# The front's work in another order: q copied three steps ahead, k'v one step sooner, gating begun once its tiles are done

## The chip, the cores and the metric

The kernel runs on one core of a Trainium2 chip. The core has a matrix engine (TensorE, PE in the rows; PEld is its load of weights), VectorE (DVE), ScalarE (ACT), GpSimd (POOL) and SyncE (SP), which only issues DMAs here. Each engine works off its own queue strictly in order and waits for the others through semaphores. The metric is the device time of one execution in microseconds, lower is better.

## The reference

```python
# attention: 4 batches, 8 heads, 576 rows, head dimension 64, float32
kv  = einsum('bhsd,bhse->bhde', k, v)
out = einsum('bhsd,bhde->bhse', q, kv)
out = out / sqrt(mean(out*out, -1) + 1e-6) * g_norm
x   = out.transpose(0, 2, 1, 3).reshape(2304, 512)
# mixture of experts: 8 experts, width 1024, the best two of each row
noisy = x @ w_gate + log1p(exp(x @ w_noise)) * noise
x = sum over the two best e of  weight_e * (relu(x @ w1[e]) @ w2[e])
# MLP of width 2048
h = maximum(x @ w_in, 0)
out = (s * h*h + b) @ w_out
```

## The kernel before

The 2304 rows are 18 tiles of 128. The program has two parts. The **front** does the attention, the norm and the gating and writes normalised rows to a table xs in HBM. The **main part** gathers the rows of each expert from xs, multiplies, and ends with the MLP. Every product of the main part is made of three fp32r matmuls (L815 to L817 and L839 to L841), with each operand split into a high and a low part (xh and xl, w1h and w1l, w2h and w2l, hh and hl).

The order of work is written out by hand: each engine's queue holds its instructions in the order in which the code emits them, and SyncE's DMAs go out in that order too. The change is all in the front, which runs over ten chunks, or **steps**, c = 0 to 9. A step has two tiles, or one (steps 4 and 9, which hold the last 64 rows of two batches each). Steps 0 and 1 are batch 0, 2 and 3 batch 1, 5 and 6 batch 2, 7 and 8 batch 3; step 4 needs batches 0 and 1, step 9 batches 2 and 3. What is emitted for a chunk:

- **repack(c)** copies q of chunk c into qc, heads in the order of the transposes: on ScalarE for odd c, on VectorE for even c (L398, L400). **q_tr(c)** transposes qc on TensorE (L410, into qtp), and ScalarE evicts to qT (L412).
- **kv(b)** multiplies k' by v of batch b (L334) and ScalarE evicts to kvc (L339). **kv_put(b)** copies kvc into the block-diagonal kvbd on VectorE (L345). **mfold_a(b)** transposes kvc (L352, evicted to kvT, L354); **mfold_b(b)** multiplies it by the gate's weights (L361) and ScalarE puts the result beside kv in kvbd (L364). att of a batch needs both.
- **att(c, u)** multiplies qT by kvbd for tile u (L423), and **evict(c, u)** takes it to x on ScalarE (L432). **squares(c)** (sq, ScalarE, L438), **sums(c)** (ss, VectorE, L445; iw, GpSimd, L447), **inv_rms(c)** (iv, two ScalarE instructions, L457 and L458) and **norm(c)** (six VectorE instructions, L469 to L479: iu twice, iv, x's gate columns, the logits lg, the normalised xn) make the norm. **put_rows** writes xn to xs with a DMA on SyncE (L487).
- **advance(n)**, from step 6 on, loads expert weights on SyncE and splits n units: w1h and w2h on ScalarE, w1l on VectorE, w2l on GpSimd (L154).

**Gating** of the first nine tiles is a generator that tick() moves on. Each tick either runs its next piece or counts down the number that the last piece yielded; norm has five ticks, one behind each of its last five instructions (iu is two), sums has one. Its pieces: gate_noise (two ScalarE, two GpSimd instructions, from lg; yields 2), gate_choice twice (six VectorE instructions each, beginning with m_all, L518; 1 each), a pause of 6, gate_rank (matmuls; 1), the one-hots (nine VectorE instructions, L540; 6), the matmuls of the list of rows (L546; 1), the list idx_e (VectorE, L550) and two gathers from xs on GpSimd (L187; 11), and put_x for the two blocks gathered: four transposes (L371), xh on ScalarE (L374), xl on VectorE (L375). What is left at the end of the front is run at once by finish_chain. Then the first expert's matmuls start (L815 to L817).

Tiles rotate through buffers: x has two (a chunk's evict waits for norm of the chunk two before it), xn three (norm waits for the DMA of the chunk three before), q, k and v two batches each (a load waits for the last reader), qc and qT two, qtp one.

Of the kernel before, what the change touches and what calls it, by code (L numbers as in the profile page):

```python
# [8 lines left out]
F32 = mybir.dt.float32  # L9
# [12 lines left out]
def kernel(  # L22
# [18 lines left out]
    P = 128  # L41
    B, H, S, D = q.shape
# [23 lines left out]
    HW_ = D + W2C  # L66
# [146 lines left out]
    pool = front.__enter__()  # L213
# [4 lines left out]
    def small_ps(shape):  # L218
        p_, tag, bufs = small[0]
        return p_.tile(shape, F32, name="sps", tag=tag, bufs=bufs)  # L220
# [4 lines left out]
    def load_kv(b, m0=0, m1=NM):  # L225
        for nm, src in (("k", k), ("v", v)):
            sv = src[b].rearrange("h s d -> (h s d)").rearrange("(m r x) -> r m x", r=P, x=KJ * D)
            if m0 == 0:
                KQV[b, nm] = pool.tile([P, NM, KJ, D], F32, name=nm, bufs=2)
            nc.sync.dma_start(KQV[b, nm].rearrange("p m j d -> p m (j d)")[:, m0:m1], sv[:, m0:m1])  # L230


    def load_q(b):
        KQV[b, "q"] = pool.tile([P, H, NJ, D], F32, name="q", bufs=2)
        nc.sync.dma_start(KQV[b, "q"].rearrange("p h j d -> p h (j d)"),
                          q[b, :, :SM].rearrange("h (p j) d -> p h (j d)", j=NJ))
        if b % 2 == 0:
            KQV[b // 2, "qr"] = pool.tile([P, H, D], F32, name="qr", bufs=2)
        o = SR * (b % 2)
        nc.sync.dma_start(KQV[b // 2, "qr"][o:o + SR], q[b, :, SM:].rearrange("h p d -> p h d"))  # L240
# [101 lines left out]
    def kv_put(b):  # L342
        for m in range(2):
            r = slice(m * D, (m + 1) * D)
            nc.vector.tensor_copy(kvbd[b][r, :, :, m, :D], KVP[b][1][r])  # L345


    def mfold_a(b):
        kvc = KVP[b][1]
        pt = small_ps([P, 2, P])  # L350
        for a in range(2):
            nc.tensor.transpose(pt[:, a, :], kvc[:, a].rearrange("p i d -> p (i d)"), ident)  # L352
        kvT = pool.tile([P, 2, P], F32, name="kvT", bufs=1)
        nc.scalar.activation(kvT, pt, AF.Copy)  # L354
        KVP[b] = kvT

    def mfold_b(b):
        kvT = KVP[b]
        pm = small_ps([P, 2, 2, 2, W2C])
        for a in range(2):  # L360
            nc.tensor.matmul(pm[:, a], lhsT=kvT[:, a, :], rhs=gw[:, a], start=True, stop=True)  # L361
        for m in range(2):
            r = slice(m * D, (m + 1) * D)
            nc.scalar.activation(kvbd[b][r, :, :, m, D:], pm[r, :, m], AF.Copy)  # L364
# [12 lines left out]
    QC, QT, AT, XC, XO = {}, {}, {}, {}, []  # L377
# [8 lines left out]
    def repack(c):  # L386
        if c >= NCH:
            return
        t0, n = CHUNKS[c]
        qc = QC[c] = pool.tile([P, 2, 2, 2, 2, D], F32, name="qc", bufs=2)  # L390
        for u in range(n):
            tl = TILES[t0 + u]
            src = KQV[tl[0], "q"][:, :, tl[1], :] if n == 2 else KQV[tl[0] // 2, "qr"]
            src = src.rearrange("p (a m i) d -> p i a m d", a=2, m=2)
            for i in range(2):
                dst = qc[:, u, :, i]
                if c % 2:
                    nc.scalar.activation(dst, src[:, i], AF.Copy)  # L398
                else:
                    nc.vector.tensor_copy(dst, src[:, i])  # L400

    def q_tr(c):
        if c >= NCH:
            return
        t0, n = CHUNKS[c]
        qc = QC.pop(c).rearrange("p u a i m d -> p u (a i) (m d)")
        pt = fps.tile([P, 2, 4, P], F32, name="qtp", bufs=1)
        for u in range(n):
            for g in range(4):
                nc.tensor.transpose(pt[:, u, g, :], qc[:, u, g, :], ident)  # L410
        qT = pool.tile([P, 2, 4, P], F32, name="qT", bufs=2)
        nc.scalar.activation(qT[:, :n], pt[:, :n], AF.Copy)  # L412
        QT[c] = qT
# [14 lines left out]
    def evict(c, u):  # L428
        t0, n = CHUNKS[c]
        if u == 0:  # L430
            XC[c] = (pool.tile([P, 2, H, HW_], F32, name="x", bufs=2),)
        nc.scalar.activation(XC[c][0][:, u].rearrange("p (a h) c -> p a h c", a=2), AT.pop(t0 + u), AF.Copy)  # L432

    def squares(c):
        x, = XC[c]
        n = CHUNKS[c][1]
        sq = pool.tile([P, 2, H, D], F32, name="sq", bufs=1)
        nc.scalar.activation(sq[:, :n], x[:, :n, :, :D], AF.Square)  # L438
        XC[c] = (x, sq)

    def sums(c):
        x, sq = XC[c]
        n = CHUNKS[c][1]
        ss = pool.tile([P, 2, H], F32, name="ss", bufs=2)
        nc.vector.tensor_reduce(ss[:, :n], sq[:, :n], axis=AX, op=OP.add)  # L445
        w = pool.tile([P, 2, H], F32, name="iw", bufs=2)
        nc.gpsimd.tensor_scalar(w[:, :n], ss[:, :n], -0.5 / D, -0.5e-6, op0=OP.mult, op1=OP.add)  # L447
        tick()
        XC[c] = (x, ss, w)

    def inv_rms(c):
        if c < 0:
            return
        x, ss, w = XC[c]
        n = CHUNKS[c][1]
        y = pool.tile([P, 2, H], F32, name="iv", bufs=2)
        nc.scalar.activation(y[:, :n], ss[:, :n], AF.Ln, scale=1.0 / D, bias=eps)  # L457
        nc.scalar.activation(y[:, :n], y[:, :n], AF.Exp, scale=-0.5)  # L458
        XC[c] = (x, w, y)

    def norm(c):
        if c < 0:
            return
        x, w, y = XC.pop(c)
        t0, n = CHUNKS[c]
        x, w, y = x[:, :n], w[:, :n], y[:, :n]

        u = pool.tile([P, 2, H], F32, name="iu", bufs=2)[:, :n]
        nc.vector.tensor_mul(u, y, y)  # L469
        nc.vector.tensor_mul(u, u, w)  # L470
        tick()
        nc.vector.scalar_tensor_tensor(y, u, 1.5, y, op0=OP.add, op1=OP.mult)
        tick()
        nc.vector.tensor_mul(x[:, :, :, D:], x[:, :, :, D:], y[:, :, :, None].to_broadcast([P, n, H, W2C]))
        tick()
        nc.vector.tensor_reduce(lg[:, t0:t0 + n, :], x[:, :, :, D:].rearrange("p n h c -> p n c h"), axis=AX, op=OP.add)
        tick()
        xn = pool.tile([P, 2, H, D], F32, name="xn", bufs=3)[:, :n]
        nc.vector.tensor_mul(xn, x[:, :, :, :D], y[:, :, :, None].to_broadcast([P, n, H, D]))  # L479
        tick()  # L480
        XO.append((t0, n, xn))

    def put_rows():
        if not XO:
            return
        t, n, x = XO.pop(0)
        nc.sync.dma_start(xs[t * P:(t + n) * P, :].rearrange("(n p) d -> p n d", n=n), x.rearrange("p n h d -> p n (h d)"))  # L487
# [9 lines left out]
    def gate_noise(g):  # L497
        t0, t1 = GROUPS[g]
        T = t1 - t0
        ex = gate_tmp(g, [P, T, E])  # L500
        nc.scalar.activation(ex, lg[:, t0:t1, E:], AF.Exp)
        nc.scalar.activation(ex, ex, AF.Ln, bias=ones1)
        nl = gate_tmp(g, [P, T, E])
        nc.gpsimd.tensor_mul(nl, ex, nz[:, t0:t1, :])
        nc.gpsimd.tensor_add(nl, nl, lg[:, t0:t1, :E])
        GT[g] = (nl, gate_tmp(g, [P, T, E]), gate_tmp(g, [P, T, E], BF16))
        yield 2
# [92 lines left out]
    def gating(g):  # L600
        yield from gate_noise(g)
        yield from gate_choice(g, 0)
        yield from gate_choice(g, 1)
        yield 6
        yield from gate_rank(g)
        yield from gate_slots(g)
# [4 lines left out]
    def tick():  # L611
        if chain[0] is None:
            return
        if chain[1] > 1:
            chain[1] -= 1
            return
        chain[1] = next(chain[0], None)
        if chain[1] is None:
            chain[0] = None
# [115 lines left out]
    repack(1)  # L735
    q_tr(1)
    load_q(2)

    KV_AT = {1: 1, 3: 2, 6: 3}

    for c, (t0, n) in enumerate(CHUNKS):
        new = KV_AT.get(c)
        for u in range(n):
            att(c, u)
            evict(c, u)
            if u == 0:
                inv_rms(c - 1)
        if new:
            kv(new)
        squares(c)  # L750
        repack(c + 2)
        q_tr(c + 2)
        if new:
            kv_put(new)
            mfold_a(new)
        norm(c - 1)
        put_rows()
        sums(c)
        if new:
            mfold_b(new)  # L760
        if c == 1:
            load_kv(3)
            load_q(3)
        if c and sum(CHUNKS[c - 1]) == NT0:
            chain[:] = [gating(0), 0]
        if c >= 6:
            advance(c - 6)
    inv_rms(NCH - 1)
# [345 lines left out]
```

## Time and profile before

| | |
|---|---|
| time of three runs | 1008.91 us median (1008.45 to 1009.35) |
| the profiled execution | 1007.86 us, span of its trace 1006.1 us |
| PE matmul busy | 948.1 us, 94% of the span |
| DVE, ACT, POOL busy | 530.0, 397.3 and 109.8 us |
| DMA | 129.03 MB, mean 128 GB/s |

The span runs from the first to the last instruction. Busy time is the time in which an engine had an instruction in work; a matmul's end is modelled. In a row of a timeline, "x4" says that several like instructions are merged, and the bracket at the end gives how long the engine stood idle before it and what released it.

### The profile page before, as it was taken

To read this page: it belongs to the slowest core of one execution; us is meant where nothing else is said; L and a number is where in the kernel's file an instruction comes from. 1 tells how busy PE (TensorE), PEld (TensorE's weight loads), DVE (VectorE), ACT (ScalarE), POOL (GpSimd) and SP (SyncE) were. 2 spreads that over 40 slices of the span, in tenths; PEclk is the share of its full clock that TensorE was granted. 3 is DMA by queue.
4 is the path that set the end of the run, shared out by engine and by line. 5 is a ranking of instruction groups with operands and counts; after the bars stand their busy time and mean duration, and the time that the engine had idled before them with its cause. 6 is when DMAs were issued, how large, how long until landed. Compare 5 with 4: busy or idle time off the path is not lost.

```text
span 1006.1 us, 14220 instructions
## 1 busy us (share of the span) xinstructions
PE 948.1 (94%) x5530; PEld 821.8 (82%) x5531; DVE 530.0 (53%) x976; ACT 397.3 (39%) x708; POOL 109.8 (11%) x128
## 2 busy tenths in 40 slices
PE   6763799999999999999999999999999999999997
PEld 4753688888999999999998998888878878887886
DVE  1458667554576776776745565434434443443333
ACT  2565243433464565555534443322223232222222
POOL 2002134300010010000000112100110011000000
PEclk8787699999999999999999999999999999999999
DMA  9824386825478466675635532200120012001001
GB/s 287 288 90 157 107 261 198 274 72 182 136 231 280 148 219 211 215 260 170 224 116 189 177 128 82 74 11 1 36 91 1 22 47 58 1 1 42 1 1 42
DMA packets 103354, 129.03 MB, mean 128 GB/s; under 512 B 9808, under 2 KB 68176, under 8 KB 103280
## 3 DMA queue, kind: packets, MB, share of 16 engines
q1 hardware_dynamic: 95856, 108.02, 32.6%
q0 software_dynamic: 6208, 20.00, 6.9%
q8 instruction: 44, 0.72, 0.3%
q14 instruction: 30, 0.25, 0.1%
q10 hardware_dynamic: 1216, 0.03, 0.1%
HBM read 92.91 MB, written 35.13 MB: 127 GB/s over the span
## 4 chain that ended last, share of the span: by engine, by line
PE 75%; DVE 1%; ACT 1%; issue 0%; ACTq 0%
PE ph L816 12%; PE ph L817 12%; PE ph L815 12%; PE y L839 12%; PE y L840 12%; PE y L841 12%; PE sps L371 2%; DVE r L825 0%; ACT hh L827 0%; ACT r L824 0%; DVE r L826 0%; DVE xl L375 0%; DVE hl L828 0%; DVE rows L848 0%; ACT xh L374 0%
## 5 line engine op out<-in xcount | busy, mean ns | idle before, releaser
L816 PE MATMUL ph<-xl,w1h 128*128 128x320 f32 (+3 forms) x832 | 278.2, 334 | 2.8 <-DVE xl L375 2.7
L817 PE MATMUL ph<-xh,w1l 128*128 128x320 f32 (+3 forms) x832 | 277.9, 334 | 2.9 <-DVE w1l L148 2.9
L815 PE MATMUL ph<-xh,w1h 128*128 128x320 f32 (+3 forms) x832 | 278.0, 334 | 2.1 <-ACT xh L374 1.2
L839 PE MATMUL y<-w2h,hh 128*128 128x512 f32 x608 | 243.4, 400 | 2.9 <-ACT hh L827 2.1
L840 PE MATMUL y<-w2l,hh 128*128 128x512 f32 x608 | 238.4, 392 | 0.0
L841 PE MATMUL y<-w2h,hl 128*128 128x512 f32 x608 | 238.2, 392 | 0.0
L816 PEld LDWEIGHTS ph<-xl,w1h 128*128 128x128 f32 x832 | 158.2, 190 | 18.5 <-DVE xl L375 5.1
L815 PEld LDWEIGHTS ph<-xh,w1h 128*128 128x128 f32 x832 | 158.2, 190 | 18.3 <-ACT xh L374 3.4
L817 PEld LDWEIGHTS ph<-xh,w1l 128*128 128x128 f32 x832 | 158.2, 190 | 12.9 <-DVE w1l L148 3.1
L819 ACT ACTIVATE hh<-ph 128x320 fp32r<-128x320 f32 (+2 forms) x128 | 55.9, 437 | 232.2 <-PE ph L817 219.9
L825 DVE SCALAR_TENSOR_TENSOR r<-ph,r 128x512 f32<-128x512 f32 (+1 forms) x80 | 51.1, 638 | 178.1 <-ACT r L824 174.0
L820 DVE SCALAR_TENSOR_TENSOR hl<-ph,hh 128x320 fp32r<-128x320 f32 (+2 forms) x128 | 62.4, 489 | 148.4 <-ACT hh L819 141.9
L841 PEld LDWEIGHTS y<-w2h,hl 128*128 128x128 f32 x608 | 114.6, 188 | 25.4 <-DVE hl L828 0.6
L839 PEld LDWEIGHTS y<-w2h,hh 128*128 128x128 f32 x608 | 114.9, 189 | 24.3 <-ACT hh L827 2.7
L840 PEld LDWEIGHTS y<-w2l,hh 128*128 128x128 f32 x608 | 115.0, 189 | 20.4
L824 ACT ACTIVATE r<-ph 128x512 f32<-128x512 f32 (+1 forms) x80 | 44.4, 556 | 190.0 <-PE ph L817 183.5
L827 ACT ACTIVATE hh<-r 128x512 fp32r<-128x512 f32 (+1 forms) x80 | 47.1, 589 | 101.6 <-DVE r L826 99.3
L828 DVE TENSOR_TENSOR hl<-r,hh 128x512 fp32r<-128x512 f32 (+1 forms) x80 | 51.1, 639 | 52.5 <-ACT hh L827 49.7
L187 POOL DMA_INDIRECT rows<-xs,idx x35 | 34.4, 982 | 314.5 <-PE sps L371 191.9
L187 POOL DMA_INDIRECT rows<-ys,slot_i x36 | 35.0, 971 | 272.5 <-DVE rows L797 136.3
L148 DVE SCALAR_TENSOR_TENSOR w1l<-raw,gcol,w1h 128x512 fp32r<-128x512 f32 x64 | 47.7, 747 | 22.1 <-ACT w1h L146 17.6
L153 ACT ACTIVATE w2h<-raw 128x512 fp32r<-128x512 f32 x80 | 49.7, 621 | 5.5 <-DMA raw<-in_moe_w_dram 5.4
(165 smaller groups left out, 807.3 us busy)
## 6 DMA issues: line engine op xcount, KB each, us to landing
raw<-in_moe_w_dram SPq DMA_DIRECT2D x128, 256.0 KB
ys<-rows SPq DMA_DIRECT2D x40, 256.0 KB
c_raw<-in_moe_w_in_dram SPq DMA_DIRECT2D x16, 512.0 KB
c_raw<-in_moe_w_out_dram SPq DMA_DIRECT2D x16, 512.0 KB
wd<-c_fl SPq DMA_DIRECT2D x16, 512.0 KB
raw<-wd SPq DMA_DIRECT2D x32, 256.0 KB
ys<-zero SPq DMA_DIRECT2D x13, 512.0 KB
q<-in_q_dram SPq DMA_DIRECT2D x4, 1024.0 KB
```

The source lines that it names most:

```text
L153: nc.scalar.activation(h2, r2, AF.Copy)
L187: nc.gpsimd.indirect_dma_start(out=dst, out_offset=None, in_=src, in_offset=bass.IndirectOffsetOnAxis(ap=icol, axis=0))
L815: nc.tensor.matmul(ps[:, :wd], lhsT=w1h[:, c, :], rhs=xh[:, c, cs], start=c == 0, stop=False)
L816: nc.tensor.matmul(ps[:, :wd], lhsT=w1h[:, c, :], rhs=xl[:, c, cs], start=False, stop=False)
L817: nc.tensor.matmul(ps[:, :wd], lhsT=w1l[:, c, :], rhs=xh[:, c, cs], start=False, stop=c == KC - 1)
L819: nc.scalar.activation(hh[:, cs], ps[:, :wd], AF.Relu)
L820: nc.vector.scalar_tensor_tensor(hl[:, cs], ps[:, :wd], 0.0, hh[:, cs].bitcast(F32), op0=OP.max, op1=OP.subtract)
L825: nc.vector.scalar_tensor_tensor(r[:, :wd], ps[:, :wd], 0.0, r[:, :wd], op0=OP.max, op1=OP.mult)
L828: nc.vector.tensor_sub(hl[:, cs], r[:, :wd], hh[:, cs].bitcast(F32))
L839: nc.tensor.matmul(y, lhsT=hh[:, cs], rhs=w2h, start=f == 0, stop=False)
L840: nc.tensor.matmul(y, lhsT=hh[:, cs], rhs=w2l, start=False, stop=False)
L841: nc.tensor.matmul(y, lhsT=hl[:, cs], rhs=w2h, start=False, stop=f == nf - 1)
```

## The change

x gets a third buffer. repack(2) is emitted ahead of the loop, and step c copies chunk c+3 behind its q_tr(c+2), where it copied chunk c+2 ahead of it. kv(b) is emitted in steps 0, 3 and 5 (before: 1, 3 and 6), behind squares in place of ahead of it, and mfold_b(b) one step after kv(b), behind that step's att. The loads of batch 3 are issued in step 0 ahead of put_rows, where they were at the end of step 1. Gating is started in step 5 ahead of sums, with one tick of its own, where it was started behind sums.

```diff
     def evict(c, u):
         t0, n = CHUNKS[c]
         if u == 0:
-            XC[c] = (pool.tile([P, 2, H, HW_], F32, name="x", bufs=2),)
+            XC[c] = (pool.tile([P, 2, H, HW_], F32, name="x", bufs=3),)
...
     load_q(2)
-
-    KV_AT = {1: 1, 3: 2, 6: 3}
+    repack(2)
+
+    KV_AT = {0: 1, 3: 2, 5: 3}
 
     for c, (t0, n) in enumerate(CHUNKS):
-        new = KV_AT.get(c)
+        new, last = KV_AT.get(c), KV_AT.get(c - 1)
         for u in range(n):
             att(c, u)
             evict(c, u)
             if u == 0:
                 inv_rms(c - 1)
+        if last:
+            mfold_b(last)
+        squares(c)
         if new:
             kv(new)
-        squares(c)
-        repack(c + 2)
         q_tr(c + 2)
+        repack(c + 3)
         if new:
             kv_put(new)
             mfold_a(new)
+        if c == 0:
+            load_kv(3)
+            load_q(3)
         norm(c - 1)
         put_rows()
-        sums(c)
-        if new:
-            mfold_b(new)
-        if c == 1:
-            load_kv(3)
-            load_q(3)
         if c and sum(CHUNKS[c - 1]) == NT0:
             chain[:] = [gating(0), 0]
+            tick()
+        sums(c)
         if c >= 6:
             advance(c - 6)
```

## Rows read from the trace of the kernel before

**Rows 1.** Busy us by stretch: total, PE, PEld, DVE, ACT, POOL, clock, DMA, GB/s

```profile
27.20:107.00 79.80, 48.58 (x687) 42.92 (x687) 50.78 (x121) 43.60 (x93) 10.14 (x17) 0.78 0.55 181
...
107.00:1006.10 899.10, 881.92 (x4643) 767.17 (x4643) 475.62 (x836) 345.71 (x600) 92.12 (x90) 0.99 0.37 119
```

**Rows 2.** Waits of VectorE, 27 to 107 us: total, times, longest

```profile
DVE kvbd L345 <- ACT kvc L339: 13.5, 3, 6.2
...
DVE iu L469 <- ACT iv L458: 9.3, 4, 4.7
DVE xl L375 <- ACT xh L374: 1.9, 1, 1.9
DVE m_all L518 <- POOL g L505: 1.8, 1, 1.8
```

**Rows 3.** Waits of TensorE for copied q, same stretch and columns

```profile
PE qtp L410 <- ACT qc L398: 13.8, 4, 6.1
```

**Rows 4.** Timeline, steps 0 to 5: start, duration, instruction, idle before

```profile
25.71 0.70 ACT L432 ACTIVATE x<-att 128x640 f32<-128x640 f32 x1 [0.38 <-PE att L423]
...
27.22 0.90 DVE L400 COPY qc<-q 128x256 f32<-128x256 f32 x4 [9.72 <-DMA q<-in_q_dram]
...
32.49 2.44 PE L334 MATMUL sps<-v,k 64*64 64x64 f32 x144
...
35.44 0.59 DVE L345 COPY kvbd<-kvc 64x256 f32<-64x256 f32 x2 [6.19 <-ACT kvc L339]
...
41.44 4.03 PE L423 MATMUL att<-kvbd,qT 128*128 128x160 f32 x16 [0.64 <-issue]
...
45.13 0.17 DVE L469 TENSOR_TENSOR iu<-iv 128x16 f32<-128x16 f32 x1 [4.67 <-ACT iv L458]
...
50.87 0.59 DVE L345 COPY kvbd<-kvc 64x256 f32<-64x256 f32 x2 [1.72 <-ACT kvc L339]
```

**Rows 5.** Timeline, steps 6 and 7

```profile
73.27 0.59 DVE L345 COPY kvbd<-kvc 64x256 f32<-64x256 f32 x2 [5.56 <-ACT kvc L339]
...
76.78 0.23 DVE L518 TENSOR_REDUCE m_all<-g 128x9 f32<-128x72 f32 x1 [1.76 <-POOL g L505]
...
81.36 1.21 DVE L445 TENSOR_REDUCE ss<-sq 128x16 f32<-128x1024 f32 x1
...
83.19 0.17 DVE L469 TENSOR_TENSOR iu<-iv 128x16 f32<-128x16 f32 x1 [0.62 <-ACT iv L458]
...
85.99 1.21 DVE L445 TENSOR_REDUCE ss<-sq 128x16 f32<-128x1024 f32 x1
...
87.59 2.87 DVE L540 TENSOR_SCALAR ohe<-io,early 128x256 f16<-128x256 f16 x9
```

**Rows 6.** Timeline, end of the front, start of the first expert

```profile
95.84 1.27 POOL L154 TENSOR_TENSOR w2l<-raw,w2h 128x512 fp32r<-128x512 f32 x1
...
95.94 1.21 DVE L470 TENSOR_TENSOR iu<-iu,iw 128x16 f32<-128x16 f32 x1
...
97.07 0.15 DVE L550 TENSOR_SCALAR idx_e<-sps 128x2 int32<-128x2 f32 x1
...
97.50 1.27 POOL L187 DMA_INDIRECT rows<-xs,idx_e  x1 [0.38 <-DVE iv L472]
...
99.07 1.34 POOL L187 DMA_INDIRECT rows<-xs,idx_e  x1 [0.30 <-issue]
...
101.04 1.21 DVE L470 TENSOR_TENSOR iu<-iu,iw 128x8 f32<-128x8 f32 x1
...
104.52 1.09 PE L371 MATMUL sps<-ident,rows 128*128 128x128 f32 x4 [2.10 <-DMA rows<-xs,idx_e]
...
107.02 0.58 PE L816 MATMUL ph<-xl,w1h 128*128 128x256 f32 x1
```

**Rows 7.** SyncE's queue of DMA issues

```profile
38.96 0.37 SPq L487 DMA_DIRECT2D xs<-xn  x1
...
41.60 4.03 SPq L240 DMA_DIRECT2D qr<-in_q_dram  x1
```

## Prediction

> **What bounds the kernel now.** I read the busy times by stretch first. After 107 us TensorE is busy 881.9 of 899.1 us at a granted clock of 0.99 [rows 1]: the experts and the MLP are bound by their matmuls, and no instruction in them changes. They start when the first gathered rows have been turned into xh and xl; the first matmul that reads xl (L816) begins at 107.02 [rows 6]. So the question is only when that moment comes. Before it, from 27.2 to 107, no engine is full: TensorE 48.6, VectorE 50.8, ScalarE 43.6 of 79.8 us [rows 1]. The time goes into handing over.
>
> VectorE has the most work there and ends last, so I keep its account: its waits in that stretch add up to 13.5 (kvbd, for kvc) + 9.3 (iu, for iv) + 1.9 (xl) + 1.8 (m_all) = 26.5 us; the 9.72 for q ended at 27.22 [rows 2, 4]. Busy 50.8 + waits 26.5 = 77.3; the other 2.5 us are short gaps between its 121 instructions, which I keep. What the change can give is in those 26.5 us.
>
> Where they come from: step 1 lasts from 29.4 to att(2) at 41.44 [rows 4]. TensorE does att(1), then k'v of batch 1 at 32.49; q_tr(3) waits for a copy of q that ScalarE makes only after kvc and squares; then come mfold_a and mfold_b, and only then att(2). TensorE waited 13.8 us in four such places for copied q [rows 3]. VectorE meanwhile stood 6.19 us before kvbd and 4.67 before iu [rows 4]; step 6 repeats it (5.56) [rows 5]. After 76.8 its waits are short (0.62 before iu at 83.19, 1.9 before xl [rows 2, 5]): there the others wait for it.
>
> **The change part by part.** No instruction and no transfer is added or removed but for a third x buffer. Every term is a wait that goes, stays or comes. I laid each engine's queue out in the new order, an instruction starting when its engine is free and its inputs are there, with the durations of the trace (TensorE's between its two clocks: 1.1 times the fast ones). The old order laid out so has att(2) at 41.2 and L816 at 106.5, where the trace has 41.44 and 107.02 [rows 4, 6]; I trust it to about 1 us.
>
> *q copied three steps ahead.* repack(2) still waits for q to land at 27.2. From repack(3) on, the copy is made a step before its transposes, in time that ScalarE has free (43.6 of 79.8 us busy); TensorE's 13.8 us go. Without that cover each copy would cost its 0.9 to 1.3 us again.
>
> *k'v one step sooner.* kv(1) runs on TensorE after att(0), whose second evict starts at 25.71, while q is still under way: 25.7 to 28.2 (2.44 us by its row). kvc is there when VectorE leaves repack(2) at 28.1, and the wait of 6.19 goes. As ss(0) ends at 30.0 and iv comes after the next evict, which stands behind qT(2) and repack(3) on ScalarE, norm(0) starts at 33.1: a new wait of 2.7. mfold_b now follows the next step's att and no longer waits for kvT ahead of it. att(2) moves from 41.4 to 34.1.
>
> In the steps that follow, VectorE runs norm (2.8 us, from 83.19 to 85.99) and ss (1.2), and then waits for one round trip: ss ends at 82.57, the next norm starts at 83.19, 0.62 us [rows 5]. I count 0.7 in front of norm(1), (3), (5) and (6): 2.8, where the row of iu had 9.3.
>
> kv_put still stands ahead of norm on VectorE, so norm and ss wait behind it, and x's buffer with them. In step 3 kvc(2) comes after sq(3), at 44.6, and VectorE is free at 42.7: 1.9 (before 1.72 [rows 4]). In step 5 att(5) starts at 50.2, kvc(3) is there at 56.1, VectorE free at 54.1: 2.0 (before 5.56).
>
> *x in three buffers.* ScalarE waited in places for xn to free x. In the new layout this is worth nothing: the same step's inv_rms waits for a later VectorE instruction anyway. Without it the layout ends at the same time; the bound is one evict, 0.7 us.
>
> *Gating begun sooner.* gate_noise now runs at the end of step 5; ScalarE waits there for lg(4), to 58.3, with evict(6) behind it: 0.5 us, off VectorE's path. Its results are on hand at 59.8, VectorE comes to the choice at 61.0, and the 1.76 before m_all [rows 5] go. The one-hots (2.87 [rows 5]) move ahead of xn(6): same work, earlier, and x waits for them. The list of rows is ready at 80.0 in place of 97.07, and the gathers go out at 80.2 and 81.5. The second one's rows reached TensorE 5.45 us after its issue (99.07 to 104.52 [rows 6]), so by 87.0; VectorE reaches put_x after lg(9), at 91.0. The gather is hidden with 4 us to spare, the 1.9 before xl goes, and xl stands ahead of xn(9). The price: iw(8) is now queued behind both gathers (1.27 + 1.34 us [rows 6]) on GpSimd, and norm(8) waits for it: 1.4.
>
> *VectorE and GpSimd.* The two-input L470 took 1.21 us at 95.94 and ended as w2l did (95.84 + 1.27); its like took 0.17, and L470 at 101.04 again 1.21 [rows 5, 6]. So two were held. Now all three splits in the front fall on a norm, since the one-hots no longer cover the first: a third hold, 1.0 to 1.1; bounds 0 and 1.27.
>
> The Trainium skill, "SBUF — State Buffer", section "Who interferes with whom", says that a VectorE instruction with two SBUF inputs and a GpSimd instruction that reads SBUF share a read port, and that the later one is blocked until the first ends. The trace agrees: 1.21 against 0.17 us. By it the third hold costs 1.1; if the splits missed the norms, as one did before, the sum would be 1.1 us better.
>
> *SyncE.* The loads of k, v, q of batch 3 now go out ahead of the first xs write, which before was issued at 38.96, right ahead of them; the last of them took 4.03 us to issue at 41.60 [rows 7]. They start at about 30, when kv(1) and repack(3) have freed the buffers, land by about 48, and nothing needs them before 51. xs(0) goes out behind them at about 41 and should have landed near 50; norm(3) needs its xn buffer at about 51.5. Bounds: nothing, or 4.5 us if it lands as late as 56. I take nothing.
>
> **Sum.** Waits 26.5 before; after, 2.7 + 2.8 + 1.9 + 2.0 + 1.4 = 10.8, and 1.1 more for holds. Gain 26.5 - 10.8 - 1.1 = 14.6 us: L816 at 92.4. From there the experts are shifted as they are: their loads are issued relative to their own steps, and three weight units are split beforehand as now. Span 1006.1 - 14.6 = 991.5; the profiled run 1007.86 - 14.6 = 993.3; the median of the runs shown is 1.05 above that run, so **994.3**.
>
> **The rivals.**
> *Half of it* (0.18). The waits for kvc, behind which all of norm stands, stay as they were: 13.5 in place of 3.9, gain 5.0, 1003.9; the late xs(0) alone would give 998.8. For it: kv_put has not moved on VectorE, and step 3 keeps its wait by my own account. Against it: TensorE no longer waits for q ahead of kv.
> *More* (0.10). The splits miss the norms and iw(8) is not late: another 2 to 3 us, about 991; with the 2.7 of norm(0) gone too, 989. For it: before, one split in three missed. No more than 26.5 us can go at all.
> *It does not do what it says* (0.05). The waits come back elsewhere on VectorE, which has 50.8 + 2.5 us of work at the least, or the experts wait for weights what the front has saved: 1008 to 1010. For it: SyncE's weight loads in the front wait for VectorE's norm. Against it: those move along with it.
> *Slower* (0.05). The experts start after a longer stretch in which TensorE is idle, and run at the lower clock for longer. The front has a mean granted clock of 0.78, the rest 0.99 [rows 1]. A stretch of t us at half the clock costs t/2, so it eats the gain when the lower level lasts 29 us longer than now; 35 us give 1012. Against it: the matmuls that follow are dense as before.
>
> **Numbers.** The forecast holds 0.62. Under 0.2% (2 us) a measurement of this kernel can't be told from no change. Faster: 0.62 + 0.18 + 0.10 = 0.90; same 0.05; slower 0.05. The forecast's own range is 991 to 998 (1 us for the layout, 0 to 4.5 for xs(0), about 2.5 the other way). With "more" down to 989 and most of "half of it" up to 1003, the range is 989 to 1003.
>
> **What would show it.** att(2) at about 34 in place of 41.4, att(7) at 61 to 62; no wait over 1 us for copied q after step 1; kvbd's waits near 0, 2 and 2; the gathers issued about 80, with put_x not waiting for a DMA; L816 near 92. If xn waits for a DMA in step 4, the order on SyncE did it; if kvbd's waits stay over 5, the first rival; if L816 comes early and the end does not follow, the third.

## The result, and the profile after

The changed kernel took 993.87 us (median of four runs, 991.76 to 996.30), the kernel before 1008.68 beside it: a ratio of 0.9855 [0.9831, 0.988], so about 14.6 us faster (14.8 by the medians). The forecast was 994.3. The profiled execution took 993.72 us with a span of 991.9; the prediction had 991.5 for the span. Line numbers up to the loop are as before; behind it they are 2 higher, so the matmul that reads xl is L818 where it was L816.

The windows of the changed kernel come first, cut at the moments that answer to [rows 1] (the start of repack(2), the first matmul that reads xl, the end); the columns are as there.

```profile
26.68:93.46 66.78, 42.47 (x612) 36.63 (x603) 50.21 (x120) 43.13 (x93) 9.93 (x17) 0.82 0.67 214
93.46:991.90 898.44, 881.58 (x4643) 766.93 (x4643) 476.20 (x837) 346.49 (x600) 92.02 (x90) 0.99 0.37 119
```

The main part takes what it took: 898.4 us after 899.1, at the same clock. The front is 13.0 us shorter (66.8 after 79.8), and VectorE's work in it is nearly the same (50.2 after 50.8). So the time came out of waits, as told, and nothing of it was given back by the experts. Of the 14.2 us between the two spans, 1.2 lie outside the front: repack(2) starts 0.5 us sooner, and the main part is 0.7 shorter.

VectorE's waits in that stretch (total, times, longest), to set against [rows 2]:

```profile
DVE iu L469 <- ACT iv L458: 5.6, 5, 3.1
DVE kvbd L345 <- ACT kvc L339: 4.5, 3, 2.0
DVE qc L400 <- PE qtp L410: 2.8, 1, 2.8
DVE iu L470 <- issue: 1.0, 1, 1.0
DVE iv L472 <- DVE iu L470: 0.3, 1, 0.3
```

They add up to 14.2 us (the wait for q ahead of 26.68 is left out as before), where they were 26.5. The 1.0 that the view calls "issue" ends when GpSimd's iw(8) does, at 85.0; in other runs of this order the view names it (L447). The waits for m_all and for xl are gone. One line is new, and the prediction has nothing like it: VectorE waits 2.8 us to copy q, for TensorE's transposes. The timeline of steps 0 to 2 shows where (start, duration, instruction, idle before and releaser, as in [rows 4]):

```profile
25.35 2.33 PE L334 MATMUL sps<-v,k 64*64 64x64 f32 x144
...
27.61 0.66 PE L410 MATMUL qtp<-ident,qc 128*128 128x128 f32 x4
...
28.21 0.59 DVE L345 COPY kvbd<-kvc 64x256 f32<-64x256 f32 x2 [0.63 <-ACT kvc L339]
...
31.68 1.11 PE L410 MATMUL qtp<-ident,qc 128*128 128x128 f32 x4 [3.42 <-issue]
...
32.84 0.49 DVE L400 COPY qc<-qr 128x256 f32<-128x256 f32 x2 [2.79 <-PE qtp L410]
...
36.42 0.17 DVE L469 TENSOR_TENSOR iu<-iv 128x16 f32<-128x16 f32 x1 [3.09 <-ACT iv L458]
...
37.42 2.41 PE L423 MATMUL att<-kvbd,qT 128*128 128x160 f32 x16
```

kv(1) runs in step 0 and its kvbd waits 0.63 us, where that wait was 6.19. q_tr(2) then stops in its middle: four of its eight transposes run, TensorE does nothing for 3.42 us, and the profile finds no instruction that it waited for ("issue"). All eight read what VectorE had copied by 27.6. q_tr(2) ends 3.4 us later for it, VectorE's copy of the last 64 rows of batches 0 and 1 (into the buffer that q_tr(2) frees) waits 2.79 us, and att(2) comes at 37.42 where the prediction had 34.1.

The rest of the front, from the start of gating to the first expert:

```profile
61.54 0.26 ACT L501 ACTIVATE g<-lg 128x72 f32<-128x72 f32 x1 [0.64 <-DVE lg L476]
...
64.23 0.22 DVE L518 TENSOR_REDUCE m_all<-g 128x9 f32<-128x72 f32 x1
...
73.38 1.85 DVE L540 TENSOR_SCALAR ohe<-io,early 128x256 f16<-128x256 f16 x9
...
81.94 0.15 DVE L550 TENSOR_SCALAR idx_e<-sps 128x2 int32<-128x2 f32 x1
...
83.76 0.98 POOL L187 DMA_INDIRECT rows<-xs,idx_e  x1 [0.30 <-issue]
...
85.10 1.26 POOL L154 TENSOR_TENSOR w2l<-raw,w2h 128x512 fp32r<-128x512 f32 x1
...
85.26 1.13 DVE L472 SCALAR_TENSOR_TENSOR iv<-iu,iv 128x16 f32<-128x16 f32 x1
...
89.05 1.09 PE L371 MATMUL sps<-ident,rows 128*128 128x128 f32 x4 [0.47 <-DMA rows<-xs,idx_e]
...
92.13 1.28 DVE L375 TENSOR_TENSOR xl<-sps,xh 128x512 fp32r<-128x512 f32 x2
...
93.46 0.58 PE L818 MATMUL ph<-xl,w1h 128*128 128x256 f32 x1 [2.06 <-DVE xl L375]
```

m_all has its input when VectorE comes to it. The nine one-hots take 1.85 us in place of 2.87 [rows 5]. The second block's rows reach TensorE 5.3 us after the gather was issued, and VectorE takes both xl without a wait.

### The profile page after: what moved, and what is told of

It reads as the page before. It is cut to its first block, busy times and chain, and to the rows that moved or that the text cites. A ratio compares the mean times of both kernels' runs of the same rounds, so it can differ in the third digit from the quotient of the medians.

```text
span 991.9 us, 14216 instructions
## 1 busy us (share of the span) xinstructions
PE 943.4 (95%) x5530; PEld 818.1 (82%) x5531; DVE 530.1 (53%) x976; ACT 397.3 (40%) x708; POOL 109.5 (11%) x128
## 4 chain that ended last, share of the span: by engine, by line
PE 76%; DVE 1%; ACT 1%; issue 0%; ACTq 0%
PE ph L818 13%; PE ph L819 13%; PE ph L817 12%; PE y L841 12%; PE y L843 12%; PE y L842 12%; PE sps L371 2%; DVE r L827 0%; ACT hh L829 0%; ACT r L826 0%; DVE r L828 0%; DVE xl L375 0%; DVE hl L830 0%; DVE rows L850 0%; ACT xh L374 0%
## 5 line engine op out<-in xcount | busy, mean ns | idle before, releaser
L818 PE MATMUL ph<-xl,w1h 128*128 128x320 f32 (+3 forms) x832 | 278.2, 334 | 4.7 <-DVE xl L375 4.7
L818 PEld LDWEIGHTS ph<-xl,w1h 128*128 128x128 f32 x832 | 158.0, 190 | 20.5 <-DVE xl L375 6.9
```

Of the source, the lines that this page charges most:

```text
L818: nc.tensor.matmul(ps[:, :wd], lhsT=w1h[:, c, :], rhs=xl[:, c, cs], start=False, stop=False)
```

## The experiments

All ratios are to the kernel before on the same chip, with 95% intervals. Executions start their loads a little earlier or later, so the profiled runs are compared by the stretch from repack(2) on VectorE to the first matmul that reads xl ("front" below). That is one execution of each kernel; the two of the changed kernel differ by 1.3 us:

| kernel | repack(2) | first xl matmul | front, us | ratio |
|---|---|---|---|---|
| before | 27.22 | 107.02 | 79.8 | 1 |
| changed | 26.68 | 93.46 | 66.8 | 0.9855 [0.9831, 0.988] |
| changed, again | 25.13 | 90.66 | 65.5 | 0.9859 [0.984, 0.9878] |
| copy_only | 26.29 | 96.51 | 70.2 | 0.9897 [0.9879, 0.9915] |
| kv_only | 25.58 | 98.97 | 73.4 | 0.9919 [0.9904, 0.9934] |
| gate_only | 27.16 | 108.01 | 80.9 | 0.9997 [0.9986, 1.0009] |
| gate_late | 26.78 | 100.95 | 74.2 | 0.9931 [0.9915, 0.9946] |
| x_two | 26.06 | 94.01 | 68.0 | 0.9876 [0.9855, 0.9898] |
| load2_late | 26.50 | 95.53 | 69.0 | 0.9871 [0.9847, 0.9895] |
| load2_wait | 25.82 | 93.74 | 67.9 | 0.9869 [0.9852, 0.9886] |
| load2_pool | 26.82 | 95.30 | 68.5 | 0.9872 [0.9851, 0.9893] |
| low_dve | 27.66 | 93.30 | 65.6 | 0.9867 [0.9846, 0.9889] |
| put_late | 27.04 | 90.19 | 63.2 | 0.9832 [0.981, 0.9855] |
| put_late_load2 | 25.93 | 88.76 | 62.8 | 0.9813 [0.9791, 0.9835] |

### One part alone

**The copies alone, three steps ahead, in the kernel before.**

```diff
     load_q(2)
+    repack(2)
...
-        repack(c + 2)
         q_tr(c + 2)
+        repack(c + 3)
```

> The kernel before with q alone copied three steps ahead. My theory (VectorE's waits for what TensorE and ScalarE hand over are what goes, and the parts share them): TensorE no longer waits for copied q ahead of its transposes, so most of the way to the whole gain: 8 to 10 us of the 14.6, some 1000 us, kvbd's wait of 5 to 6 us shrinks as steps get shorter, the gather is still waited for. Rival (each part has its own waits, and they add up): a third or less, 1004 us.

It gave 994.43 us, 0.9897: 10.5 us, just above the 8 to 10 expected. VectorE's waits in its front, to set against [rows 2]:

```profile
DVE kvbd L345 <- ACT kvc L339: 9.3, 3, 6.0
DVE iu L469 <- ACT iv L458: 3.1, 3, 1.8
DVE m_all L518 <- POOL g L505: 2.4, 1, 2.4
DVE xl L375 <- ACT xh L374: 2.0, 1, 2.0
```

TensorE's waits for copied q are gone, and with them most of VectorE's waits for iv (3.1 after 9.3). The wait for kvc in step 1 stays at 6.0: the copies do not free it. Some of that 6.0 is a stop of TensorE of 1.6 us inside kv(1), which a later section takes up.

**k'v alone, one step sooner, its folds spread.**

```diff
-    KV_AT = {1: 1, 3: 2, 6: 3}
+    KV_AT = {0: 1, 3: 2, 5: 3}
...
-        new = KV_AT.get(c)
+        new, last = KV_AT.get(c), KV_AT.get(c - 1)
...
+        if last:
+            mfold_b(last)
+        squares(c)
         if new:
             kv(new)
-        squares(c)
...
-        if new:
-            mfold_b(new)
```

> The kernel before with k'v one step sooner and mfold_b behind the next step's att, alone. My theory: also 6 to 9 us by itself, 1000 to 1003 us, so that the two parts done singly give more together than the whole change, because both shorten the same steps. Rival: 4 us or less, as the copy of q still holds TensorE.

It gave 996.58 us, 0.9919: 8.4 us. Here it is the other way round: kvbd waits 5.7 us in all and 2.7 at most, iu 9.0 in all and 4.5 at most, and TensorE's waits for copied q are back at 14.7. The two parts take different waits, each mainly what the prediction gave it: the copies those for iv, k'v those for kvc.

**Gating alone, begun sooner, in the kernel before.**

```diff
+        if c and sum(CHUNKS[c - 1]) == NT0:
+            chain[:] = [gating(0), 0]
+            tick()
         sums(c)
...
-        if c and sum(CHUNKS[c - 1]) == NT0:
-            chain[:] = [gating(0), 0]
```

> The kernel before with gating begun sooner, alone. Taken out of the changed kernel, it cost some 7 us. Theory (its worth there is that copies of q and k'v, moved sooner on ScalarE, stood ahead of gate_noise and kept VectorE waiting; without them there is little to win): within 2 us of the kernel before, on either side. Rival (the parts add up, and gating sooner hides the gather by itself): 5 to 7 us faster than the kernel before.

It gave 1005.16 us beside 1005.76: 0.9997 [0.9986, 1.0009], no change. The waits before m_all and xl do go (1.8 and 1.9 us, [rows 2]), but VectorE now waits 1.9 for the matmuls that rank the tiles (L565) and 1.0 for iw(8) behind the gathers. It comes to m_all at 76.79, as before (76.78), though it no longer waits there: kvbd's waits are 2.0 longer, 1.3 of it in step 3, ahead of any gating, in a stretch in which this execution had the lower clock for longer (0.73 from 40 to 55 us, where the kernel before had 0.84). TensorE stops in it as well, for 1.71 us inside kv(1), though the order up to there is that of the kernel before, whose trace has no such stop:

```profile
34.59 0.56 PE L334 MATMUL sps<-v,k 64*64 64x64 f32 x20 [1.71 <-issue]
```

**The changed kernel with gating begun as before.**

```diff
-        if c and sum(CHUNKS[c - 1]) == NT0:
-            chain[:] = [gating(0), 0]
-            tick()
         sums(c)
+        if c and sum(CHUNKS[c - 1]) == NT0:
+            chain[:] = [gating(0), 0]
```

> The changed kernel with gating begun where the kernel before begins it. My theory: VectorE's list of rows and the gathers come a step later and the gather's way (5 us) stands again ahead of xl: 2 to 3 us slower than the changed kernel, 996 to 997 us. Rival (gating is hidden in any case, the gain is all in the steps): no difference.

It gave 998.16 us, 0.9931 beside 0.9855 and 0.9859: about 7 us, more than twice what I had expected. The profiled execution took 999.24. Its timeline in steps 6 to 9:

```profile
66.45 1.06 ACT L438 ACTIVATE sq<-x 128x1024 f32<-128x1024 f32 x1
...
68.46 0.71 ACT L398 ACTIVATE qc<-qr 128x256 f32<-128x256 f32 x2
...
69.07 0.25 ACT L501 ACTIVATE g<-lg 128x72 f32<-128x72 f32 x1
...
70.58 0.23 DVE L518 TENSOR_REDUCE m_all<-g 128x9 f32<-128x72 f32 x1 [3.92 <-POOL g L505]
...
98.45 1.09 PE L371 MATMUL sps<-ident,rows 128*128 128x128 f32 x4 [2.34 <-DMA rows<-xs,idx_e]
...
100.20 0.69 DVE L375 TENSOR_TENSOR xl<-sps,xh 128x512 fp32r<-128x512 f32 x1 [2.02 <-ACT xh L374]
```

The logits that gate_noise reads were done at 63.2 (lg, 62.82 + 0.37). But gate_noise is emitted behind squares, qT and the copy of step 6, and ScalarE reaches it at 69.07: VectorE waits 3.9 us for m_all. The list then comes too late to cover the second gather (2.0 before xl), and the one-hots fall beside a w2l again (2.89 us in place of 1.85). kvbd waits 2.4 us more, mostly for an att(5) that took 4.47 us at the lower level of the clock (0.50 granted from 53 to 58 us in this execution, 1.00 in the changed kernel's, where att(5) took 2.3). The waits for qc and for iw(8) are 1.0 each shorter. That is 3.9 + 2.0 + 2.4 - 1.0 - 1.0 = 6.3 us of waits and 0.8 of work (51.0 after 50.2), of the 7.4 by which the front is longer. Whether gating late makes the clock fall there, or this execution had it by chance, is not shown; the 3.9 and the 2.0 do not hang on it.

So the three parts are worth 10.5, 8.4 and 0 us alone, 14.6 together, and only 6.8 (1004.96 - 998.16) without the third. The first two together (with the x buffer and the sooner loads) give less than either alone: against copy_only, VectorE waits 2.4 less for kvc here, but 2.6 more for iv, 1.5 more for m_all and 1.8 for the stop in q_tr(2). The earlier the rest of the step, the later stands an unmoved gate_noise: 1.8 us of wait before, 2.4 with the copies, 3.2 with k'v, 3.9 with both.

**x with two buffers in the changed kernel.**

```diff
-            XC[c] = (pool.tile([P, 2, H, HW_], F32, name="x", bufs=3),)
+            XC[c] = (pool.tile([P, 2, H, HW_], F32, name="x", bufs=2),)
```

> The changed kernel with x in two buffers again. My account gave the third buffer nothing: within 0.5 us of the changed kernel (0.9855 of the kernel before), and ScalarE waits for xn of the chunk two before for no more than the wait for ss that comes right behind it. Rival (the third buffer carries the gain of the later steps, where ScalarE waited 4.9 us for xn): 2 us or more slower, 0.988 or above.

It gave 992.62 us, 0.9876 [0.9855, 0.9898]. ScalarE now waits 6.7 us in three places for xn to free x, and 5.3 for ss where it waited 12.9; VectorE's waits are nearly the same (iu 6.0, kvbd 5.0). So the waits fit the account: one wait of ScalarE stands in for another. The time settles neither the theory nor the rival: by the ratios it lies 2 us above the changed kernel's, and the intervals overlap.

### The stop in q_tr(2)

The same stop stands in every kernel in which TensorE gets that far early, and always behind the same number of matmuls, in whatever order they are. Counted from the end of att(0), it falls in the changed kernel behind kv(1) (144) and four transposes, in copy_only and gate_only, where q_tr(2) and att(1) come first, behind 8 + 16 and 124 matmuls of kv(1): 148 each time.

In copy_only:

```profile
29.93 2.08 PE L334 MATMUL sps<-v,k 64*64 64x64 f32 x124
33.63 0.56 PE L334 MATMUL sps<-v,k 64*64 64x64 f32 x20 [1.61 <-issue]
```

A place that goes by the count of instructions and not by data suggests the fetching of the program itself. The DMA view of the changed kernel from 29 to 30 us (packets, MB, share of 16 engines' time) has one packet of an instruction queue among the loads:

```profile
DMA packets 164, 0.38 MB, mean 383 GB/s; under 512 B 4, under 2 KB 4, under 8 KB 163
...
q1 hardware_dynamic: 163, 0.37, 97.8%
q8 instruction: 1, 0.02, 6.5%
```

Over the whole run that queue has 44 packets:

```profile
q8 instruction: 44, 0.72, 0.3%
```

That is 16 KB each. TensorE runs 5530 matmuls and 5531 weight loads in this kernel, 251 to a packet; the 976, 708 and 128 instructions of VectorE, ScalarE and GpSimd are far too few for 44 packets at that rate. So the queue is most likely TensorE's own.

The times agree. In the changed kernel the packet starts to cross at 29.08 us and TensorE goes on at 31.68, 2.60 us later. In the twelve executions that have the stop, TensorE goes on 2.4 to 2.8 us behind the start of the packet. In the kernel before, the packet starts at 31.75 and TensorE comes to that matmul at 34.4, 2.6 us later, so that nothing is left to wait for.

The theory: TensorE waits for a block of its instructions, which comes through the same DMA engines as the loads of k, v and q, and behind them. The rival: the stop has its own cause in the order of work (a buffer or a semaphore that the profile does not show), and is there with the DMA engines idle too. The tests move the loads of batch 2, that fill the engines then.

**Loads of batch 2 written down later**, in step 0.

```diff
-    load_kv(2)
     mfold_a(0)
...
-    load_q(2)
     repack(2)
...
         if c == 0:
+            load_kv(2)
+            load_q(2)
             load_kv(3)
```

> The changed kernel with the loads of k, v and q of batch 2 issued in step 0, behind kv(1) and q_tr(2), in place of ahead of the loop. In the changed kernel TensorE stood 3.4 us in the middle of q_tr(2), at 28.3 to 31.7, for nothing that the profile shows; a packet of instructions landed between 29 and 30, while the queues were full of loads. Theory: TensorE waited for its own instructions, which come behind the loads; with the rings empty there the stop is under 1 us, att(1) starts about 29.5 in place of 32.8, and up to 2.5 us are gained (991.5 us), as batch 2 is needed only at 39. Rival: the stop is no matter of the loads (TensorE waits for a semaphore): it stays at 3.4 us, and the time is the same, or longer if batch 2 then comes late.

It gave 991.84 us, 0.9871, and the stop is 2.89 us. But it tests nothing: SyncE had nothing else to issue before them, ran ahead of the other engines, and issued the first of these loads at 19.4 us all the same.

**The loads held back by the tile rotation**, with a dummy allocation ahead of load_kv(2).

```diff
+    for nm in ("k", "v"):
+        pool.tile([P, NM, KJ, D], F32, name=nm, bufs=2)
     load_kv(2)
```

> The changed kernel with the loads of batch 2 really held back: its k and v take the buffers of batch 1, so that SyncE waits for kv(1) before it issues them (the earlier try left SyncE's queue as it was, since nothing in front of these loads had changed, and says nothing). TensorE stopped in all five kernels so far behind the same instruction of its queue (164 matmuls from the start of att(0)), wherever the order put it, which speaks for a block of instructions that has not come. Theory: the block comes late because the rings are full of loads; with nothing in them from about 27.5 to 28.5 it lands sooner, the stop falls from 3.4 to under 1.5 us, att(1) starts near 30.5 and 1 to 2.5 us are gained. Rival: the block's way does not depend on the loads: stop as before, and the time the same or up to 2 us longer, as batch 2 and 3 land some 2 us later.

Nor did this hold them: k of batch 2 went out at 18.48 us, and the stop is 3.43 us; 991.25 us, 0.9869.

**The loads of batch 2 on GpSimd's queue**, behind its iw of step 0, and those of batch 3 at the end of step 1 again.

```diff
-    load_kv(2)
     mfold_a(0)
...
-    load_q(2)
     repack(2)
...
-        if c == 0:
-            load_kv(3)
-            load_q(3)
...
         sums(c)
+        if c == 0:
+            dq[0] = nc.gpsimd
+            load_kv(2)
+            load_q(2)
+            dq[0] = nc.sync
+        if c == 1:
+            load_kv(3)
+            load_q(3)
```

> The changed kernel with the loads of batch 2 issued from GpSimd's queue behind iw(0), and those of batch 3 at the end of step 1 as in the kernel before, so that no load is in the rings from the landing of q of batch 1 (about 27) to some 30 us. (Holding batch 2 back through its buffers had left SyncE's issues where they were, at 18.5 us.) Theory: TensorE's stop behind the 164th matmul is a block of instructions that comes late because it shares the DMA engines with the loads: the stop, 2.6 to 3.5 us in every run of this order so far, falls under 1.5 us. Rival: the way of the block is as long in an empty ring: the stop stays over 2.5 us. The time is no test here: batch 2 and 3 come later and iw(1) stands behind four DMA issues; I expect the changed kernel's time or 1 to 4 us more.

Now the loads go out from 31.24 us, and before that the DMA engines run empty: 73 GB/s from 25 to 26 us, the last of q of batch 1, and no load from 27 to 31. TensorE in step 0 and 1, and the DMA view from 25 to 26 us:

```profile
25.93 2.33 PE L336 MATMUL sps<-v,k 64*64 64x64 f32 x144
28.19 1.09 PE L412 MATMUL qtp<-ident,qc 128*128 128x128 f32 x8
...
29.34 2.34 PE L425 MATMUL att<-kvbd,qT 128*128 128x160 f32 x16
```

```profile
q1 hardware_dynamic: 141, 0.06, 30.5%
q8 instruction: 1, 0.02, 7.0%
```

All eight transposes run in one piece. The packet starts at 25.67, 0.3 us before kv(1) does, where in the changed kernel it started 3.7 us behind the start of kv(1) (25.35); TensorE comes to the fifth transpose at 28.7, 3.0 us after the packet. So the rival is out: the order of work is the same up to there, and the stop is gone. The kernel is no faster for it, 992.61 us and 0.9872, since the late loads cost it elsewhere: VectorE's copies wait 3.7 us more for q to land, and ScalarE's 5.5.

### The waits that the prediction left in place

**kv_put behind norm on VectorE.** kvc is taken to kvbd one norm later, so that norm and ss no longer stand behind the wait for it.

```diff
             KVP[b] = ps, kvc
+            KVC[b] = kvc
...
-            nc.vector.tensor_copy(kvbd[b][r, :, :, m, :D], KVP[b][1][r])
+            nc.vector.tensor_copy(kvbd[b][r, :, :, m, :D], KVC[b][r])
...
         if new:
-            kv_put(new)
             mfold_a(new)
...
         put_rows()
+        if new:
+            kv_put(new)
```

> The changed kernel with kv_put behind norm on VectorE (kvc kept by name, nothing else moved). Theory (what stands on VectorE's path counts one for one): the waits of 1.8 and 2.0 us for kvc in steps 3 and 5 go, as norm runs in that time: 2 to 3.5 us faster than the changed kernel. Rival: norm then waits for iv in place of kvc, or att(5) and att(7) for kvbd: within 0.5 us of the changed kernel.

It gave 987.82 us, 0.9832. The changed kernel ran again beside it, unchanged:

> The changed kernel once more, unchanged, as the mark for the others of this set. Theory: about 0.9855 times the kernel before again, with TensorE standing some 3 us in the middle of q_tr(2). Rival: the stop was a chance of one execution, and is not there.

That gave 990.23 us, 0.9859. VectorE's waits in the front of put_late (lines are 1 higher):

```profile
DVE iu L470 <- ACT iv L459: 6.1, 5, 3.1
DVE qc L401 <- PE qtp L411: 2.9, 1, 2.9
DVE iu L471 <- POOL iw L448: 1.0, 1, 1.0
DVE kvbd L346 <- ACT kvc L339: 0.5, 1, 0.5
```

kvbd's waits fall from 3.8 (in the run beside it) to 0.5, no other grows by more than 0.6, and the front is 2.4 us shorter. So these two waits of 1.8 and 2.0 us could be taken away by an order, and what went did not come back elsewhere on VectorE. The time alone, 2.4 us less than the run beside it, does not prove it: the two intervals overlap.

**The front's three w2l on VectorE**, where GpSimd had them.

```diff
-    low_engine = [nc.gpsimd]
+    low_engine = [nc.vector]
...
             advance(c - 6)
+    low_engine[0] = nc.gpsimd
     inv_rms(NCH - 1)
```

> The changed kernel with w2l of the three units that are split in the front made on VectorE in place of GpSimd. Theory: the three holds of 1.0 us each on norm's two-input instructions go, VectorE has three more instructions of 0.68 us (its time for the same w2l later in the trace): 1 us faster than the changed kernel, and no L470 or L472 over 0.2 us in the front. Rival: the long L470 has nothing to do with GpSimd: it stays at 1.2 us and the time grows by 2 us.

VectorE's groups in its front (total, mean ns of one):

```profile
L154 DVE TENSOR_TENSOR w2l<-raw,w2h 128x512 fp32r<-128x512 f32 x3 | 2.1, 688 | 0.0
L470 DVE TENSOR_TENSOR iu<-iu,iw 128x16 f32<-128x16 f32 (+1 forms) x10 | 1.7, 174 | 1.4 <-POOL iw L447 0.5
L472 DVE SCALAR_TENSOR_TENSOR iv<-iu,iv 128x16 f32<-128x16 f32 (+1 forms) x10 | 1.7, 173 | 0.5 <-DVE iu L470 0.3
```

All ten L470 and all ten L472 now take 0.17 us, where one L472 took 1.13 and two L470 1.2: the three holds were GpSimd's w2l and nothing else. They cost 3.0 us together and the three w2l cost VectorE 2.1; the gain of 1 us that I expected did not show (991.26 us, 0.9867, after 990.23; the front 65.6 us as in the run beside it).

**Both: kv_put behind norm, and the loads of batch 2 held until kv(1) has read batch 1's tiles**, into which they are then written.

The edit is that of put_late and this:

```diff
-            if m0 == 0:
+            if b == 2:
+                KQV[b, nm] = KQV[1, nm]
+            elif m0 == 0:
                 KQV[b, nm] = pool.tile([P, NM, KJ, D], F32, name=nm, bufs=2)
...
-    load_kv(2)
     mfold_a(0)
...
-    load_q(2)
     repack(2)
...
         if c == 0:
+            load_kv(2)
+            load_q(2)
             load_kv(3)
```

> Two findings together: kv_put behind norm, and the loads of batch 2 held until kv(1) is done by writing its k and v over those of batch 1 (all from SyncE's queue, batch 3 right behind). Theory: TensorE's stop behind the 164th matmul is gone (q_tr(2) in one piece, att(1) within 4 us of kv(1)'s start), the waits for kvc in steps 3 and 5 are gone, and batches 2 and 3 land early enough; from repack(2) to the first matmul that reads xl 60 to 62 us, where the changed kernel took 65.5 to 66.8 and kv_put behind norm alone 63.2; about 0.980 of the kernel before. Rival: with the start 2 to 3 us sooner, step 2 or 3 waits for batch 2 instead, and the time is that of kv_put behind norm alone, 0.983.

It gave 989.84 us beside 1007.17: 0.9813 [0.9791, 0.9835], the lowest ratio of all. It is clear of the changed kernel run again (0.984 to 0.9878), and all but clear of its first set (0.9831 to 0.988). SyncE issues k of batch 2 at 26.61, and the stop shrinks to 0.49 us:

```profile
26.45 0.65 PE L413 MATMUL qtp<-ident,qc 128*128 128x128 f32 x4
27.60 0.66 PE L413 MATMUL qtp<-ident,qc 128*128 128x128 f32 x4 [0.49 <-issue]
```

```profile
DVE iu L472 <- ACT iv L461: 7.3, 6, 2.6
DVE xn L482 <- DMA xs<-xn: 1.7, 1, 1.7
```

The second fence is from VectorE's waits. VectorE comes to norm sooner and then waits more for iv (7.3 after 6.1), and the xs writes, which now stand behind the loads of two batches on SyncE, hold xn up for 1.7 us. So with hardly a stop the 2.9 us that VectorE waited for q_tr(2) are gone, and 1.7 for xn and 1.2 more for iv have come in their place: the front is 62.8 us, with put_late alone 63.2, outside the 60 to 62 expected, and the two ratios overlap. Both orders that are rid of it pay for the late loads elsewhere, so what the stop by itself costs the kernel is not measured.

## Why the prediction was right

It was right in the mechanism; that the total came within half a microsecond was in part luck. Costs that were left out or told too low, about 4 us (the stop 2.8, kvbd 0.6, norm(0) 0.4, iv 0.3), stand against 0.7 told too high in waits (iw(8) and the round trips), 1.7 in VectorE's work, and 1.3 from gaps, the start and the main part that no term of the prediction had. By its own terms, in us on VectorE:

| term | told | measured |
|---|---|---|
| kvbd's three waits | 0, 1.9, 2.0 | 0.63, 1.82, 2.01 |
| norm(0) for iv | 2.7 | 3.09 |
| round trips of norm(1), (3), (5), (6) | 4 x 0.7 | 4 x 0.62 |
| iw(8) behind the gathers | 1.4 | 1.05 |
| TensorE's stop, seen at qc | none | 2.79 |
| iv behind iu, in step 4 | none | 0.28 |
| all waits (26.5 before) | 10.8 | 14.2 |
| VectorE's work | +1.1 | -0.6 |
| short gaps, start of repack(2), main part | 0 | -0.1, -0.5, -0.7 |
| gain | 14.6 | 14.2 |

The last line for the measured column is 26.5 - 14.2 + 0.6 + 0.1 + 0.5 + 0.7.

*q copied three steps ahead*: right. TensorE has no wait for copied q any more (13.8 us before, [rows 3]), and in copy_only VectorE's wait for iv falls with it, from 9.3 to 3.1.

*k'v one step sooner*: right in each wait to 0.6 us, as the table says. The steps themselves came 3.2 to 3.3 us late from att(2) (37.42, told 34.1) to m_all (64.23, told 61.0), which is the length of the stop (3.42). That is the step which failed: "kv(1) runs on TensorE after att(0) ... while q is still under way" is so, but I let the engine go on at its own speed behind it, and TensorE stood there for 3.42 us, of which VectorE saw 2.79. The trace of before could not show it, as TensorE came to that matmul 2.6 us behind the packet; gate_only, with the same order up to there, came 1.7 us sooner and stopped. If the packet is TensorE's program, as the runs speak for, a queue laid out by hand needs the time of its landing too.

*VectorE and GpSimd*: the mis-sized term. The third hold came as told (L472 at 85.26, 1.13 us beside w2l at 85.10). What I had missed is that the one-hots had been the third hold all along: 2.87 us [rows 5] while w2l ran from 88.25 on, 1.85 with no w2l on GpSimd beside them (changed kernel, low_dve and gate_only alike). The row of w2l in the kernel before is the one below. I took their 2.87 as their price, and so counted a hold more where one was only exchanged for another: the term was 1.1, and VectorE's work fell by 0.6. The Trainium skill, "SBUF — State Buffer", section "Who interferes with whom", names tensor_scalar among the operations that can take the shared port; the 2.87 against 1.85 us agree with that.

```profile
88.25 1.33 POOL L154 TENSOR_TENSOR w2l<-raw,w2h 128x512 fp32r<-128x512 f32 x1 [0.77 <-ACT w2h L153]
```

*Gating begun sooner*: the terms were right (1.8 and 1.9 us gone). The gathers went out at 82.37 and 83.76 (told 80.2 and 81.5), the second block's rows reached TensorE at 89.05 (told 87.0), and VectorE came to xl at 92.13 (told 91.0): 3.1 us to spare and not 4, and only 1.4 from the end of the second block's xh (90.8), which xl needs as well. What gating sooner is worth inside the change is about twice what these terms say (gate_late, about 7 us), and nothing alone.

*x in three buffers* and *SyncE*: as told, as far as the runs can show. The loads of batch 3 started at 29.71 (told about 30), xs(0) went out at 41.95 (told about 41), and no xn waited for a DMA. The sooner loads of batch 3 were not run by themselves.

The rivals. *Half of it* did not come, but its mechanism was there: with the two waits behind which norm stood taken away, put_late was 2.4 us faster. *More* needed the splits to miss the norms and iw(8) to be on time; three holds fell on norm and iw(8) cost 1.05, and the 2.7 of norm(0) stayed too (3.09). *It does not do what it says* is out, with 898.4 us for the main part. *Slower* is out: the front's granted clock rose from 0.78 [rows 1] to 0.82, and the main part has 0.99 as before.

What stays open: no trace names the engine whose instructions the packet held. That it was TensorE's is concluded from the count of packets, from the fixed 2.4 to 2.8 us between the packet and TensorE going on, and from the stop that went when the loads were out of the way. Open is also what the stop costs by itself, and what the third buffer for x is worth.

## What to carry to other kernels

Take one engine that ends last, list its waits, and ask of each where it goes in the new order; the sum of what stays forecast this change within a microsecond, partly by errors that cancelled, where the parts measured alone (10.5, 8.4 and 0 us) add up to 18.9 and give the third part nothing. When work is moved up, move with it what stands in the same queue for a later stage: with gating left where it was, some 7 of 14 us were lost, 3.9 of them at m_all in the profiled execution. And before a duration is taken as the price of an operation, see what ran beside it.

## What the runs showed of the hardware

**An engine can stop, as far as these runs show, for its own program.** TensorE stood still for 3.42 and 2.66 us in two executions of the changed kernel, and for 1.61 to 3.51 in nine other kernels, while loads filled the DMA engines at some 380 GB/s; with the engines empty ahead of it, it did not stop at all in load2_pool, and 0.49 us in put_late_load2 with the loads begun late. In these twelve executions with a stop it went on 2.4 to 2.8 us after a packet of an instruction queue began to cross. The 44 packets of that queue hold 0.72 MB, 16 KB each. The Trainium skill, "Runtime: NRT & Kernel Launch", section "Instruction fetch mechanics", says that each engine's sequencer fetches its instructions in blocks of 16 KiB over a DMA queue of its own, and that the cost is mostly hidden. The size agrees; in these eleven executions with the loads ahead of it, it was not hidden. In the profile such a stop is a wait for "issue", or is put down to an instruction that ended meanwhile: in kv_only the same one (2.57 us) and in gate_late (2.70) is shown as a wait for VectorE's ss, on which no transpose depends.

```profile
29.48 0.66 PE L410 MATMUL qtp<-ident,qc 128*128 128x128 f32 x4 [2.57 <-DVE ss L445]
```

**Written order is not issue order in time.** SyncE issued the loads of batch 2 at 18.5 us (load2_wait) and 19.4 us (load2_late), as in the changed kernel (19.2), though the code has them at different places: nothing stood before them in its own queue. Written into tiles that kv(1) was still reading, they went out at 26.61 (put_late_load2).
